# Six experts' token tiles turned by VectorE blocks of 32x32 in place of TensorE transposes

## The chip, the cores and the metric

The kernel runs on one core of a Trainium2 chip. The metric is device time in microseconds (us) of one execution. Engines are named as in the profile: PE is TensorE (matmuls; PEld its weight loads), DVE is VectorE, ACT is ScalarE, POOL is GpSimd, SP is the queue of SyncE that issues most DMAs. POOL issues the indirect DMAs (gathers and scatters of rows by a list of row numbers).

## The reference, cut to what matters

```python
def reference(q, k, v, p, ...):
    a = sm_attn(q, pp, pp), pp = sm_attn(p, k, v)        # 4 batches, 8 heads, 576 tokens, 64 wide
    x = a.transpose(...).reshape(2304, 512)
    x = sum over 4 experts of p[:, e] * (relu(x @ w1[e]) @ w2[e])          # dense, 1024 hidden
    logits = x @ w_gate + log1p(exp(x @ w_noise)) * noise                  # 8 experts
    top2, weights = the two largest of 8 per token, softmax over the two
    out[token] = sum over its 2 experts of weight * (relu(x @ m1[e]) @ m2[e])
```

The change lies in the last line: each of 8 experts is run on the tokens that chose it, some 576 of 2304 on average, in a list with room for 640 (`cap`), which is 5 tiles of 128 tokens (`T2`).

## The kernel before, in words

The first 700 us are attention, the dense experts and the routing. Routing leaves in DRAM a table `meta` with one row of 4 numbers for each slot of each expert (token, weight, and two row numbers), and `x2d`, the tokens' rows of 512 numbers. The stage that the change touches is the rest of the span, the eight routed experts.

The work of this stage is cut into parts j (`subs`): expert 0 in two parts, then j = 2 is expert 1, and j = 3 to 8 are experts 2 to 7. Each part has 8 steps f, one for 128 hidden units. In a step, PE first runs `e_mm1` of the next step (24 matmuls: hidden units from the tokens' columns, two halves of 320 tokens) and then `e_mm2` of this one (15 matmuls: 5 tiles of tokens into 5 accumulators). Every product is three matmuls (`mm3`, lines 63 to 65), since numbers are split in a high part (tags ending in h) and a low part (l): ACT copies the rounded high part, and DVE or POOL subtracts it from the original (`split`, lines 68 and 69). Hidden units leave PSUM by `evac_h` (lines 468 and 469), ACT for `gh`, DVE for `gl`. Weights come as 512 KB tiles `raw` on SP, and are split into `w1h`, `w1l` and `w2h`, `w2l`: for most of the experts' weights ACT does the high and POOL the low part; DVE does the low part of some of the first ones (the list `first`).

Beside this, for the next part, `gather` (line 780) has POOL fetch 5 tiles of 128 rows of `x2d` into `xg`; and `xg_t` (line 793), for one tile in each of five steps, turns a tile over by 4 TensorE transposes (line 798) into a PSUM buffer `mm`, from which ACT and DVE split it into `xth`, `xtl`. The tile in step 6 of a part is the last one that the next part's `e_mm1` needs, and that `e_mm1` follows right behind step 6 on PE. POOL also clears (`gt`, line 804) and fills (line 808, from `yd`) the tile of what the tokens' first expert gave, and at a part's end scatters the results `y` to the output (line 851).

What goes into each engine's queue, and in which order, is set by hand: `at(place, f, ...)` gives every piece of side work a place between the PE steps, and `run` issues them there. Each engine works through its queue in order. The row numbers for the gathers come from `mt_load` (a DMA of the `meta` rows on SP) and `mt_index` (three DVE copies to integers).

Of the kernel before, what the change touches and what calls it, by code (L numbers as in the profile page):

```python
# [22 lines left out]
CH, NC = 128, 5  # L23
BIG = 65536.0
CAP = 640


@with_exitstack
def tile_pack_attn_moe_moe(ctx: ExitStack, tc: tile.TileContext, qT, kT, pT, vv, dp, noise,
# [108 lines left out]
    def at(place, f, *a):  # L138
        fill.append((place, len(fill), f, a))
# [6 lines left out]

    TM, S2 = 200, 300

    def weights(key, tag, bufs, src, load, cut):
        at(cut + 0.10, w_split, key, tag, bufs)  # L150
        at(load + 0.11, w_load, key, src)

    def w1_src(e, d):
# [580 lines left out]
    def mt_load(e0, e1, t0, t1):  # L734
        n = len(mt_i)
        m = rtp.tile([128, e1 - e0, t1 - t0, 4], F32, name="mt", tag=f"mt{n}", bufs=1)
        r0, r1 = e0 * cap + t0 * 128, (e1 - 1) * cap + t1 * 128
        ins = nc.sync.dma_start(m.rearrange("p e t c -> p (e t) c"),
                                meta[r0:r1, :].rearrange("(x p) c -> p x c", p=128))
        ix = rtp.tile([128, 3, e1 - e0, t1 - t0], I32, name="mti", tag=f"mti{n}", bufs=1)  # L740
        mt_i[n] = 0
        return m, ix, ins

    def mt_index(m, ix):
        for i, c in enumerate((0, 2, 3)):
            nc.vector.tensor_copy(ix[:, i], m[:, :, :, c])

    MT = {}

    def mt_w(e, t):  # L750
        m, _, a, b = MT[e, t]
# [13 lines left out]
    def mt_late():  # L765
        m, ix, _ = mt_load(0, 1, tA, T2)
        at(S2 + 4.1, mt_index, m, ix)
        for t in range(tA, T2):
            MT[0, t] = (m, ix, 0, t - tA)
        at(S2 + 5.3, mt_rest, 1, 2, S2 + 6.9)  # L770
        at(S2 + 13.0, mt_rest, 2, E2, S2 + 15.2)

    def mt_rest(e0, e1, place):
        m, ix, _ = mt_load(e0, e1, 0, T2)
        at(place, mt_index, m, ix)
        for e in range(e0, e1):
            for t in range(T2):
                MT[e, t] = (m, ix, e - e0, t)

    def gather(j):  # L780
        e, t0, n = subs[j]
        rows = 13 * 128 if j == 0 else NTOK
        XG[j] = [(xgp if j == 0 else mo).tile([128, 512], F32, name="xg", tag="xg", bufs=tA if j == 0 else T2)
                 for _ in range(n)]
        for t in range(n):
            ins = nc.gpsimd.indirect_dma_start(
                out=XG[j][t], out_offset=None, in_=x2d[0:rows, :],
                in_offset=bass.IndirectOffsetOnAxis(ap=mt_ix(e, t0 + t, 0), axis=0),
                bounds_check=rows - 1, oob_is_err=False)
            if j == 0:  # L790
                early_rows.append(ins)

    def xg_t(j, t):
        if t == 0:
            XT[j] = [mo.tile([128, 4, cap], F32R, name=f"xt{z}", tag=f"xt{z}", bufs=2) for z in "hl"]
        o = mm_ps()
        for d in range(4):
            nc.tensor.transpose(o[:, d * 128:(d + 1) * 128], XG[j][t][:, d * 128:(d + 1) * 128], ident)  # L798
        h, l = [z[:, :, t * 128:(t + 1) * 128] for z in XT[j]]
        split(h, l, o.rearrange("p (d j) -> p d j", d=4))  # L800

    def g_zero(e):
        Gt[e] = mo2.tile([128, T2, 512], F32, name="gt", tag="gt", bufs=1)
# [69 lines left out]
        n_over.append(nc.values_load(n_over[0][0:1, 0:1], min_val=0, max_val=NTOK))  # L873

    at(TM + 21, mt_early)
    at(TM + 26.5, gather, 0)
    for t in range(tA):
        at(TM + 36 + t, xg_t, 0, t)
    at(S2 + 2.6, mt_late)
    at(S2 + 4.12, gather, 1)  # L880
    for t in range(T2 - tA):
        at(S2 + 6.05 + t / 10, xg_t, 1, t)
    at(S2 + 10.1, count_over)
    for j in range(1, len(subs)):
        s = S2 + 8 * j
        e = subs[j][0]
        if j + 1 < len(subs):
            at(s + 0.13 if j > 1 else S2 + 7.0, gather, j + 1)
            for t in range(T2):
                at(s + 2.13 + t, xg_t, j + 1, t)  # L890
            at(s + 8.13, y_store, e)
        if e > 0:
            at(s + 2.14, g_zero, e)
            at(s + 3.14, g_load, e)
# [59 lines left out]
    with tc.If(rv > 0):  # L954
        with tc.tile_pool(name="sl", bufs=2) as sl:
            with tc.For_i(0, NT, 1) as i:
                x = sl.tile([128, 512], F32, name="sx")
                nc.sync.dma_start(x, x2d[ds(i * 128, 128), :])
                gw = sl.tile([128, E2], F32, name="sg")
                nc.sync.dma_start(gw, gwd[ds(i * 128, 128), :])  # L960
                di = sl.tile([128, 1], I32, name="sd")
                nc.sync.dma_start(di, sdd[ds(i * 128, 128), :])
                o = mm_ps()
                for d in range(4):
                    nc.tensor.transpose(o[:, d * 128:(d + 1) * 128], x[:, d * 128:(d + 1) * 128], ident)
                xt = sl.tile([128, 4, 128], F32, name="sxt")
                nc.scalar.activation(xt, o.rearrange("p (d j) -> p d j", d=4), AF.Copy)
                r = sl.tile([128, 512], F32, name="sr")
                nc.vector.memset(r, 0.0)
                for e in range(E2):  # L970
                    a = acc_ps()
                    for fp in range(4):
# [12 lines left out]
                nc.gpsimd.indirect_dma_start(out=out, out_offset=bass.IndirectOffsetOnAxis(ap=di[:, :1], axis=0),  # L985
                                             in_=r, in_offset=None, bounds_check=NTOK - 1, oob_is_err=False)


def layouts(q, k, v, p, moe_domain_probs, moe_w1, moe_w2, moe2_w_gate, moe2_w_noise, moe2_noise, moe2_w1, moe2_w2):
# [3 lines left out]
    def heads(a):  # L993
# [12 lines left out]
        ("m1", moe2_w1.reshape(E2, 4, 128, 4, 2, 128).transpose(0, 3, 2, 4, 1, 5).reshape(E2, 4, 128, 1024)),  # L1006
# [28 lines left out]
```

## Time and profile before

| | |
|---|---|
| time, median of 3 | 1237.41 us (1234.49 to 1237.69) |
| the profiled execution's own time | 1236.17 us |
| its span in the trace | 1234.3 us |
| granted TensorE clock, mean | 0.986 of full speed |
| PE busy | 1191.7 us, 97% |
| DVE, ACT, POOL busy | 437.4, 396.3 and 392.3 us |

The span runs from the first to the last instruction on the core; the execution's own time has 1.9 us more around it. The busy time of PE is modelled from pipelined instructions, so 97% says that something is always in it, not that it works at its peak.

### The profile page before, as it was taken

Reading aid. Unit: us, or ns where it says so; the run is one execution under the profiler, and the core shown is the slowest. Engines: PE = TensorE matmul, PEld = TensorE weight load, DVE = VectorE, ACT = ScalarE, POOL = GpSimd, SP = SyncE. Lnnn points to the kernel's source line nnn. Section 1 sums busy time; section 2 is a strip of 40 time slices with the busy share of each in tenths; the row PEclk is TensorE's granted clock in tenths of the full one; section 3 lists DMA queues with packets and bytes.
Section 4 is the critical chain, followed back from the end, with each engine's and each line's share of the span. In section 5 each row is a group of like instructions: output and inputs, shape, how many; then the busy total and the mean of one; then the engine's idle time right before and its main releaser. Section 6 shows DMA issues by size and latency. Waiting matters only on the chain.

```text
span 1234.3 us, 18214 instructions
## 1 busy us (share of the span) xinstructions
PE 1191.7 (97%) x7328; PEld 999.9 (81%) x7328; DVE 437.4 (35%) x1111; ACT 396.3 (32%) x848; POOL 392.3 (32%) x272
## 2 busy tenths in 40 slices
PE   6889999999999999999999988899999999999997
PEld 2668788778788888788887976689998998899986
DVE  5452343333545212633332635441222222222222
ACT  2432422323324324323223523242232323232321
POOL 0110200201203101116102143326565665757464
PEclk7999999999999999999999998899999999999999
DMA  7212131213122211301600235563344343535342
GB/s 290 100 49 116 35 111 65 77 35 112 55 104 78 74 64 35 103 1 36 104 18 18 77 90 96 131 194 99 118 138 141 111 164 111 179 98 199 100 143 78
DMA packets 50953, 121.79 MB, mean 99 GB/s; under 512 B 17658, under 2 KB 18058, under 8 KB 50864
## 3 DMA queue, kind: packets, MB, share of 16 engines
q1 hardware_dynamic: 40864, 100.46, 26.2%
q0 software_dynamic: 10000, 20.11, 5.1%
q8 instruction: 60, 0.98, 0.3%
q14 instruction: 29, 0.24, 0.1%
HBM read 106.13 MB, written 23.31 MB: 105 GB/s over the span
## 4 chain that ended last, share of the span: by engine, by line
PE 83%; DMA 6%; DVE 5%; issue 2%; ACT 2%; POOL 1%; SPq 0%; POOLq 0%; DVEq 0%; ACTq 0%
PE acc L63 13%; PE acc L64 13%; PE acc L65 13%; PE mm L63 10%; PE mm L64 10%; PE mm L65 10%; PE mm L343 2%; PE accx L63 2%; PE accx L64 2%; PE accx L65 2%; DMA gt<-yd,mti 2%; DMA meta<-rr,rsi 2%; PE mm L798 1%; DMA raw<-in_m_dram 1%; DVE ta L305 0%
## 5 line engine op out<-in xcount | busy, mean ns | idle before, releaser
L69 POOL TENSOR_TENSOR w2l<-raw,w2h 128x1024 fp32r<-128x1024 f32 x61 | 146.3, 2399 | 480.8 <-ACT w2h L68 480.5
L63 PE MATMUL acc<-w2h,hh 128*128 128x512 f32 x448 | 184.5, 412 | 0.0
L64 PE MATMUL acc<-w2l,hh 128*128 128x512 f32 x448 | 178.1, 398 | 0.0
L65 PE MATMUL acc<-w2h,hl 128*128 128x512 f32 x448 | 176.9, 395 | 0.0
L63 PE MATMUL mm<-ath,mh 128*128 128x288 f32 x512 | 153.8, 300 | 6.8 <-ACT ath L68 4.0
L63 PE MATMUL mm<-xth,w1h 128*128 128x320 f32 (+2 forms) x512 | 159.3, 311 | 0.1
L64 PE MATMUL mm<-xtl,w1h 128*128 128x320 f32 (+2 forms) x512 | 158.7, 310 | 0.3 <-DVE xtl L69 0.3
L65 PE MATMUL mm<-xth,w1l 128*128 128x320 f32 (+2 forms) x512 | 158.3, 309 | 0.0
L469 DVE SCALAR_TENSOR_TENSOR gl<-mm,gh 128x320 fp32r<-128x320 f32 (+2 forms) x128 | 62.8, 491 | 266.0 <-ACT gh L468 241.6
L469 DVE SCALAR_TENSOR_TENSOR hl<-mm,hh 128x224 fp32r<-128x224 f32 (+1 forms) x256 | 104.2, 423 | 147.8 <-ACT hh L468 144.8
L65 PE MATMUL mm<-ath,ml 128*128 128x288 f32 x512 | 151.3, 296 | 2.8 <-DVE ml L350 2.8
L64 PE MATMUL mm<-atl,mh 128*128 128x288 f32 x512 | 151.9, 297 | 0.5 <-DVE atl L69 0.4
L468 ACT ACTIVATE gh<-mm 128x320 fp32r<-128x320 f32 (+2 forms) x128 | 56.0, 437 | 285.1 <-PE mm L65 251.2
L468 ACT ACTIVATE hh<-mm 128x224 fp32r<-128x224 f32 (+1 forms) x256 | 93.3, 384 | 136.1 <-PE mm L65 105.4
L63 PEld LDWEIGHTS acc<-w2h,hh 128*128 128x128 f32 x448 | 84.1, 188 | 45.1 <-issue 29.0
L63 PE MATMUL acc<-w2h,gh 128*128 128x512 f32 x264 | 108.6, 411 | 5.7 <-ACT gh L468 5.7
L63 PEld LDWEIGHTS mm<-ath,mh 128*128 128x128 f32 x512 | 96.2, 188 | 17.9 <-ACT ath L68 6.2
L65 PE MATMUL acc<-w2h,gl 128*128 128x512 f32 x264 | 106.1, 402 | 2.1 <-DVE gl L469 2.0
L64 PE MATMUL acc<-w2l,gh 128*128 128x512 f32 x264 | 105.4, 399 | 0.0
L64 PEld LDWEIGHTS mm<-atl,mh 128*128 128x128 f32 x512 | 96.5, 188 | 6.1 <-DVE atl L69 0.9
L65 PEld LDWEIGHTS acc<-w2h,hl 128*128 128x128 f32 x448 | 84.3, 188 | 20.7
L63 PEld LDWEIGHTS mm<-xth,w1h 128*128 128x128 f32 x512 | 96.8, 189 | 3.8 <-ACT xth L68 0.4
(238 smaller groups left out, 1906.2 us busy)
## 6 DMA issues: line engine op xcount, KB each, us to landing
raw<-in_m_dram SPq DMA_DIRECT2D x72, 512.0 KB
raw<-in_w_dram SPq DMA_DIRECT2D x32, 512.0 KB
yd<-y SPq DMA_DIRECT2D x7, 1280.0 KB
w1h<-in_w_dram SPq DMA_DIRECT2D x16, 512.0 KB
w1l<-in_w_dram SPq DMA_DIRECT2D x16, 512.0 KB
v<-in_vv_dram SPq DMA_DIRECT2D x8, 640.0 KB
qk<-in_kT_dram SPq DMA_DIRECT2D x8, 576.0 KB
qk<-in_qT_dram SPq DMA_DIRECT2D x8, 576.0 KB
```

The source lines that it names most:

```text
L63: nc.tensor.matmul(o, ah, bh, start=start, stop=False)
L64: nc.tensor.matmul(o, ah, bl, start=False, stop=False)
L65: nc.tensor.matmul(o, al, bh, start=False, stop=stop)
L69: (eng or nc.vector).tensor_sub(l, x, h.bitcast(F32))
L343: nc.tensor.matmul(o[h2][hp * 32:hp * 32 + 32, :], PT[bb][r, hp, :], w, start=True, stop=True)
L468: nc.scalar.activation(hd, src, AF.Relu)
L469: nc.vector.scalar_tensor_tensor(ld, src, 0.0, hd.bitcast(F32), op0=OP.max, op1=OP.subtract)
L798: nc.tensor.transpose(o[:, d * 128:(d + 1) * 128], XG[j][t][:, d * 128:(d + 1) * 128], ident)
```

## The change

For experts 2 to 7 (`EN` = 2) a tile is gathered as four columns of quarter rows: `x2d` is seen as 9216 rows of 128 numbers, and gather b of a tile brings, to partition 32 q + i, quarter q of the token in slot 32 b + i. Four gathers of 128 rows of 512 B take the place of one of 128 rows of 2 KB. One DVE transpose of 32x32 blocks then puts the tile into the form that `e_mm1` needs, except that the rows of the contraction are permuted, which the host's layout of `m1` follows. ACT and DVE split it from SBUF (`xq`), not from PSUM.

The numbers of the quarter rows, 4 times the token plus q, are made once for all six experts: 16 small matmuls with columns of the identity put the token of slot 32 b + i on all partitions 32 q + i, and one DVE instruction multiplies by 4 and adds `quarter`. For this the load of the `meta` rows of experts 2 to 7 is placed earlier (S2 + 8.0, was S2 + 13.0), and its index instructions at S2 + 11.5 (was 15.2). The gathers of a part are placed one tile in each step, not five at once. The low parts of the weights that the second `weights` loop handles (50 tiles, from the last quarter of expert 1's on) move from POOL to DVE. A branch for tokens beyond the room of 640 is adapted as well.

```diff
+        nc.gpsimd.iota(jp, pattern=[[0, 128]], base=0, channel_multiplier=1)
+        nc.vector.tensor_scalar(jp, jp, 5, None, op0=OP.logical_shift_right)
+        nc.vector.tensor_copy(quarter, jp[:, 0:1])
...
-                weights(("m1", j, d), "w1", 2, m1[subs[j][0], d], n - 4, n - 3)
-                weights(("m2", j, d), "w2", 4, m2[subs[j][0], d], n - 3, n - 2)
+                weights(("m1", j, d), "w1", 2, m1[subs[j][0], d], n - 4, n - 3, vec)
+                weights(("m2", j, d), "w2", 4, m2[subs[j][0], d], n - 3, n - 2, vec)
...
+    def mt_index(m, ix, iq=None, eng=vec):
         for i, c in enumerate((0, 2, 3)):
+            eng.tensor_copy(ix[:, i], m[:, :, :, c])
+        if iq is not None:
+            o = mm_ps()
+            x = iq.shape[2]
+            for b in range(4):
+                for q in range(4):
+                    nc.tensor.matmul(o[q * 32:q * 32 + 32, b * x:(b + 1) * x], ident[:, b * 32:b * 32 + 32],
+                                     m.rearrange("p e t c -> p (e t) c")[:, :, 0], start=True, stop=True)
+            nc.vector.tensor_scalar(iq, o[:, :4 * x].rearrange("p (b x) -> p b x", b=4), 4.0, quarter,
+                                    op0=OP.mult, op1=OP.add)
...
-        at(S2 + 13.0, mt_rest, 2, E2, S2 + 15.2)
+        at(S2 + 8.0, mt_rest, 2, E2, S2 + 11.5)
...
+            iq, at_ = IQ[e]
+            for b in range(4):
+                nc.gpsimd.indirect_dma_start(
+                    out=XG[j][t][:, b * 128:(b + 1) * 128], out_offset=None,
+                    in_=x2d.rearrange("t (q d) -> (t q) d", q=4),
+                    in_offset=bass.IndirectOffsetOnAxis(ap=iq[:, b, at_ + t:at_ + t + 1], axis=0),
+                    bounds_check=4 * NTOK - 1, oob_is_err=False)
...
+        x = mo.tile([128, 4, 4, 32], F32, name="xq", tag="xq", bufs=2)
+        nc.vector.transpose(x.rearrange("p b d j -> p (b d j)"), XG[j][t])
+        split(*[z.rearrange("p d (b j) -> p d b j", b=4) for z in (h, l)], x.rearrange("p b d j -> p d b j"))
...
-            at(s + 0.13 if j > 1 else S2 + 7.0, gather, j + 1)
             for t in range(T2):
+                at(s + 0.13 + t if j > 1 else S2 + 7.0, gather, j + 1, (t,))
                 at(s + 2.13 + t, xg_t, j + 1, t)
```

POOL's queue over one of the experts 2 to 6, before (`w1l`, `w2l` are weight splits, `out_dram` the scatters, `xg` the gathers of tokens, `gt` the clearing and the gathers of earlier results):

```order
L851 DMA out_dram<-y,mti 2304x512 x2
L69 TENSOR_TENSOR w1l<-raw,w1h 128x1024
L851 DMA out_dram<-y,mti 2304x512 x3
L69 TENSOR_TENSOR w2l<-raw,w2h 128x1024
L786 DMA xg<-x2d,mti 128x512 x5
L69 TENSOR_TENSOR w1l<-raw,w1h 128x1024
L69 TENSOR_TENSOR w2l<-raw,w2h 128x1024
L804 MEMSET gt 128x2560
L69 TENSOR_TENSOR w1l<-raw,w1h 128x1024
L808 DMA gt<-yd,mti 128x512 x5
L69 TENSOR_TENSOR w2l<-raw,w2h 128x1024
```

The same stretch of POOL's queue in the changed kernel:

```order
L889 DMA out_dram<-y,mti 2304x512 x5
L819 DMA xg<-x2d,iq 128x128 x12
L842 MEMSET gt 128x2560
L819 DMA xg<-x2d,iq 128x128 x4
L846 DMA gt<-yd,mti 128x512 x5
L819 DMA xg<-x2d,iq 128x128 x4
```

The eight weight splits of an expert are gone from this queue, 5 gathers have become 20, and the last tile's 4 gathers now stand behind the clearing and the 5 gathers of `gt`.

DVE's queue in the changed kernel, from step 5 of an expert over step 6 to its end (`STREAM_TRANSPOSE` is the block transpose; before, a step had its two `gl` and one `xtl`):

```order
L476 SCALAR_TENSOR_TENSOR gl<-mm,gh 128x320 x2
L71 TENSOR_TENSOR w1l<-raw,w1h 128x1024
L837 STREAM_TRANSPOSE xq<-xg 128x512
L71 TENSOR_TENSOR xtl<-xq,xth 128x4x128
L476 SCALAR_TENSOR_TENSOR gl<-mm,gh 128x320 x2
L71 TENSOR_TENSOR w2l<-raw,w2h 128x1024
L837 STREAM_TRANSPOSE xq<-xg 128x512
L71 TENSOR_TENSOR xtl<-xq,xth 128x4x128
L476 SCALAR_TENSOR_TENSOR gl<-mm,gh 128x320 x2
L888 SCALAR_TENSOR_TENSOR y<-acc,mt,gt 128x512 x2
L71 TENSOR_TENSOR w1l<-raw,w1h 128x1024
L888 SCALAR_TENSOR_TENSOR y<-acc,mt,gt 128x512 x2
```

A split and a block transpose now stand in each step between the `gl` of one step and those of the next.

SP's queue around the load of the `meta` rows of experts 2 to 7 (`mt`, 128x30x4) in the changed kernel; before, it stood five rows further down, behind the fifth of the `raw` loads that follow it here:

```order
L745 DMA mt_7493<-meta_75 128x5x4
L132 DMA raw_7545<-in_m1_dram 128x1024
L132 DMA raw_7601<-in_m2_dram 128x1024
L745 DMA mt_7624<-meta_75 128x30x4
L132 DMA raw_7636<-in_m1_dram 128x1024
L132 DMA raw_7665<-in_m2_dram 128x1024
```

The load now goes out between two loads of weights for the second part of expert 0.

## Rows read from the trace of the kernel before

**Rows 1.** Part 1 of the page: busy time, share of span, instructions by engine.

```profile
PE 1191.7 (97%) x7328; PEld 999.9 (81%) x7328; DVE 437.4 (35%) x1111; ACT 396.3 (32%) x848; POOL 392.3 (32%) x272
```

**Rows 2.** Timeline of DVE, one expert: start, duration, instruction, idle time before it.

```profile
951.53 0.49 DVE L469 SCALAR_TENSOR_TENSOR gl<-mm,gh 128x320 fp32r<-128x320 f32 x1 [4.76 <-ACT gh L468]
...
958.55 0.49 DVE L469 SCALAR_TENSOR_TENSOR gl<-mm,gh 128x320 fp32r<-128x320 f32 x1 [4.77 <-ACT gh L468]
...
965.99 0.49 DVE L469 SCALAR_TENSOR_TENSOR gl<-mm,gh 128x320 fp32r<-128x320 f32 x1 [3.00 <-ACT gh L468]
...
990.06 0.49 DVE L469 SCALAR_TENSOR_TENSOR gl<-mm,gh 128x320 fp32r<-128x320 f32 x1 [1.26 <-ACT gh L468]
...
995.75 0.49 DVE L469 SCALAR_TENSOR_TENSOR gl<-mm,gh 128x320 fp32r<-128x320 f32 x1 [3.00 <-ACT gh L468]
```

**Rows 3.** Timeline of PE, same expert: a tile's four transposes, and step 6's first e_mm2.

```profile
983.35 0.60 PE L798 MATMUL mm<-ident,xg 128*128 128x128 f32 x4
...
989.39 0.39 PE L63 MATMUL acc<-w2h,gh 128*128 128x512 f32 x1
```

**Rows 4.** The chain that ended last: start us, us, what.

```profile
13.82 0.81 PE mm L271 x40
...
784.62 5.12 DMA xg<-x2d,mti
...
800.62 4.29 DMA raw<-in_m_dram
...
807.25 0.35 DVE gl L469
```

**Rows 5.** Timeline, 784 to 803 us: POOL's gathers and DVE's splits.

```profile
784.62 1.90 POOL L786 DMA_INDIRECT xg<-x2d,mti  x1 [10.93 <-DVE mti L746]
...
786.82 1.01 POOL L786 DMA_INDIRECT xg<-x2d,mti  x1 [0.31 <-issue]
787.55 1.22 DVE L69 TENSOR_TENSOR w2l<-raw,w2h 128x1024 fp32r<-128x1024 f32 x1 [1.47 <-ACT w2h L68]
...
799.38 1.22 DVE L69 TENSOR_TENSOR w2l<-raw,w2h 128x1024 fp32r<-128x1024 f32 x1
799.64 1.82 POOL L786 DMA_INDIRECT xg<-x2d,mti  x1 [0.30 <-issue]
...
801.48 1.23 DVE L69 TENSOR_TENSOR w1l<-raw,w1h 128x1024 fp32r<-128x1024 f32 x1 [0.52 <-ACT w1h L68]
801.76 1.81 POOL L786 DMA_INDIRECT xg<-x2d,mti  x1 [0.30 <-issue]
```

**Rows 6.** Groups by line, shapes apart: count | busy us, mean ns | idle before.

```profile
L69 DVE TENSOR_TENSOR xtl<-mm,xth 128x512 fp32r<-128x512 f32 x40 | 27.6, 691 | 53.6 <-ACT xth L68 50.6 <-issue 3.0
...
L325 DVE STREAM_TRANSPOSE tb<-ta 128x576 f32<-128x576 f32 x7 | 5.4, 774 | 0.4 <-POOL ta L317 0.2
```

**Rows 7.** Timeline of ACT, step 6 of the expert of rows 2.

```profile
989.93 1.05 ACT L68 ACTIVATE w2h<-raw 128x1024 fp32r<-128x1024 f32 x1
991.43 0.60 ACT L68 ACTIVATE xth<-mm 128x512 fp32r<-128x512 f32 x1 [0.45 <-PE mm L798]
```

**Rows 8.** Timeline, start of expert 1, while expert 2's tokens are fetched.

```profile
829.80 0.49 DVE L469 SCALAR_TENSOR_TENSOR gl<-mm,gh 128x320 fp32r<-128x320 f32 x1 [1.27 <-ACT gh L468]
830.80 2.38 POOL L69 TENSOR_TENSOR w2l<-raw,w2h 128x1024 fp32r<-128x1024 f32 x1 [7.88 <-ACT w2h L68]
```

**Rows 9.** Timeline of POOL, the expert of rows 2.

```profile
940.70 1.03 POOL L851 DMA_INDIRECT out_dram<-y,mti  x1 [5.48 <-DVE y L850]
...
963.64 2.24 POOL L804 MEMSET gt<- 128x2560 f32 x1
```

**Rows 10.** Windows: busy us by engine (instructions), granted clock, DMA share, GB/s.

```profile
801.00:807.00 6.00, 6.00 (x41) 5.18 (x40) 2.63 (x3) 2.16 (x4) 2.27 (x2) 1.00 0.82 283
807.00:808.00 1.00, 0.94 (x9) 0.71 (x9) 0.82 (x4) 0.38 (x1) 0.00 (x0) 1.00 0.00 0
817.00:823.00 6.00, 6.00 (x43) 5.66 (x42) 2.37 (x5) 3.01 (x5) 2.40 (x1) 1.00 0.85 155
```

More of the change, by code (lines that the diff above doesn't have):

```diff
@@ L25 @@
 CAP = 640
+EN = 2
 @with_exitstack
@@ L81, in tile_pack_attn_moe_moe @@
     cnt = consts.tile([128, 8], F32, name="cnt")
+    quarter = consts.tile([128, 1], F32, name="quarter")
     nov = consts.tile([128, NT], BF, name="nov")
@@ L147, in tile_pack_attn_moe_moe, with weights @@
     TM, S2 = 200, 300
-    def weights(key, tag, bufs, src, load, cut):
-        at(cut + 0.10, w_split, key, tag, bufs)
+    def weights(key, tag, bufs, src, load, cut, eng=None):
+        at(cut + 0.10, w_split, key, tag, bufs, eng)
         at(load + 0.11, w_load, key, src)
@@ L741, in mt_load @@
         mt_i[n] = 0
+        if e0 >= EN:
+            iq = rtp.tile([128, 4, (e1 - e0) * T2], I32, name="iq", tag=f"iq{n}", bufs=1)
+            for e in range(e0, e1):
+                IQ[e] = (iq, (e - e0) * T2)
+            return m, ix, ins, iq
         return m, ix, ins
-    def mt_index(m, ix):
+    def mt_index(m, ix, iq=None, eng=vec):
         for i, c in enumerate((0, 2, 3)):
-            nc.vector.tensor_copy(ix[:, i], m[:, :, :, c])
-    MT = {}
+            eng.tensor_copy(ix[:, i], m[:, :, :, c])
[8 more added lines that the diff above has]
+                                    op0=OP.mult, op1=OP.add)
+    MT, IQ = {}, {}
     def mt_w(e, t):
@@ L770, in mt_late @@
         at(S2 + 5.3, mt_rest, 1, 2, S2 + 6.9)
-        at(S2 + 13.0, mt_rest, 2, E2, S2 + 15.2)
+        at(S2 + 8.0, mt_rest, 2, E2, S2 + 11.5)
     def mt_rest(e0, e1, place):
-        m, ix, _ = mt_load(e0, e1, 0, T2)
-        at(place, mt_index, m, ix)
+        m, ix, _, *quarters = mt_load(e0, e1, 0, T2)
+        at(place, mt_index, m, ix, *quarters)
         for e in range(e0, e1):
@@ L778, in mt_rest, with gather @@
                 MT[e, t] = (m, ix, e - e0, t)
-    def gather(j):
+    def gather(j, ts):
         e, t0, n = subs[j]
         rows = 13 * 128 if j == 0 else NTOK
[L783 to L791, printed above, removed]
+        if ts[0] == 0:
+            XG[j] = [(xgp if j == 0 else mo).tile([128, 512], F32, name="xg", tag="xg", bufs=tA if j == 0 else T2)
+                     for _ in range(n)]
+        for t in ts:
+            if e < EN:
+                ins = nc.gpsimd.indirect_dma_start(
+                    out=XG[j][t], out_offset=None, in_=x2d[0:rows, :],
+                    in_offset=bass.IndirectOffsetOnAxis(ap=mt_ix(e, t0 + t, 0), axis=0),
+                    bounds_check=rows - 1, oob_is_err=False)
+                if j == 0:
+                    early_rows.append(ins)
+                continue
+            iq, at_ = IQ[e]
[5 more added lines that the diff above has]
+                    bounds_check=4 * NTOK - 1, oob_is_err=False)
     def xg_t(j, t):
@@ L795, in xg_t @@
             XT[j] = [mo.tile([128, 4, cap], F32R, name=f"xt{z}", tag=f"xt{z}", bufs=2) for z in "hl"]
-        o = mm_ps()
-        for d in range(4):
-            nc.tensor.transpose(o[:, d * 128:(d + 1) * 128], XG[j][t][:, d * 128:(d + 1) * 128], ident)
         h, l = [z[:, :, t * 128:(t + 1) * 128] for z in XT[j]]
-        split(h, l, o.rearrange("p (d j) -> p d j", d=4))
+        if subs[j][0] < EN:
+            o = mm_ps()
+            for d in range(4):
+                nc.tensor.transpose(o[:, d * 128:(d + 1) * 128], XG[j][t][:, d * 128:(d + 1) * 128], ident)
+            split(h, l, o.rearrange("p (d j) -> p d j", d=4))
+            return
+        x = mo.tile([128, 4, 4, 32], F32, name="xq", tag="xq", bufs=2)
+        nc.vector.transpose(x.rearrange("p b d j -> p (b d j)"), XG[j][t])
+        split(*[z.rearrange("p d (b j) -> p d b j", b=4) for z in (h, l)], x.rearrange("p b d j -> p d b j"))
     def g_zero(e):
@@ L875, in tile_pack_attn_moe_moe @@
     at(TM + 21, mt_early)
-    at(TM + 26.5, gather, 0)
+    at(TM + 26.5, gather, 0, range(tA))
     for t in range(tA):
@@ L879, in tile_pack_attn_moe_moe @@
     at(S2 + 2.6, mt_late)
-    at(S2 + 4.12, gather, 1)
+    at(S2 + 4.12, gather, 1, range(T2 - tA))
     for t in range(T2 - tA):
@@ L962, in tile_pack_attn_moe_moe @@
                 nc.sync.dma_start(di, sdd[ds(i * 128, 128), :])
[L963 to L967, printed above, removed]
+                xo = sl.tile([128, 512], F32, name="sxo")
+                nc.vector.tensor_copy(xo.rearrange("p (d q j) -> p d q j", d=4, q=4),
+                                      x.rearrange("p (q d j) -> p d q j", d=4, q=4))
+                xts = []
+                for z, y in enumerate((x, xo)):
+                    o = mm_ps()
+                    for d in range(4):
+                        nc.tensor.transpose(o[:, d * 128:(d + 1) * 128], y[:, d * 128:(d + 1) * 128], ident)
+                    xt = sl.tile([128, 4, 128], F32, name=f"sxt{z}")
+                    nc.scalar.activation(xt, o.rearrange("p (d j) -> p d j", d=4), AF.Copy)
+                    xts.append(xt)
                 r = sl.tile([128, 512], F32, name="sr")
@@ L971, in tile_pack_attn_moe_moe @@
                     a = acc_ps()
+                    xt = xts[e >= EN]
                     for fp in range(4):
@@ L1005, in layouts @@
         ("w2", moe_w2.reshape(E1, 8, 128, 512).transpose(0, 2, 1, 3)),
-        ("m1", moe2_w1.reshape(E2, 4, 128, 4, 2, 128).transpose(0, 3, 2, 4, 1, 5).reshape(E2, 4, 128, 1024)),
+        ("m1", np.concatenate([
+            moe2_w1[:EN].reshape(EN, 4, 128, 4, 2, 128).transpose(0, 3, 2, 4, 1, 5).reshape(EN, 4, 128, 1024),
+            moe2_w1[EN:].reshape(E2 - EN, 4, 4, 32, 4, 2, 128).transpose(0, 4, 1, 3, 5, 2, 6)
+            .reshape(E2 - EN, 4, 128, 1024)])),
         ("m2", moe2_w2.reshape(E2, 4, 2, 128, 512).transpose(0, 1, 3, 2, 4).reshape(E2, 4, 128, 1024)),
```

## The prediction

> **What bounds the kernel now.** I read the page's first part first: PE is busy for 97% of the span and no other engine for more than 35% [rows 1]. That only says where to look. The second view is the timeline of one of the experts 2 to 6 in its steady state. Each step leaves a pair of gl instructions on DVE, so the distance between the same gl of two neighbouring steps is the length of a step. Two steps without a tile to turn are 958.55 - 951.53 = 7.02 us apart, and the next, with a tile's four transposes, 965.99 - 958.55 = 7.44 us [rows 2]. DVE idles 3.00 to 4.77 us before these rows and waits there for ACT, which waits for PE. So in this stage PE alone sets the length of a step, and work taken from PE shortens it until something else is late.
>
> **What is removed from PE.** The trace gives the four transposes of a tile 0.60 us [rows 3], but that overlaps with the matmuls around them. The step lengths hold what they really cost: 7.44 - 7.02 = 0.42 us for a tile. Experts 2 to 7 have 6 x 5 = 30 tiles: 30 x 0.42 = 12.7 us (0.424 unrounded). All of these steps lie in the stage where PE is the bound, so this comes off the end if nothing takes its place.
>
> **What is added on PE.** 16 small matmuls for the quarter rows, once. The trace has no such form; the nearest is a run of 40 matmuls on 32 columns, 0.81 us [rows 4], which would make 0.32 us for 16. From above I take the transposes' 0.42 us for four, so 1.7 us. They are nearer to the first form: 0.5 us.
>
> **What DVE takes over.** In each step one weight split, 1.22 us [rows 5], and one block transpose, 0.69 us by the row of 774 ns for 576 columns [rows 6] scaled to 512; the low part of the tile stays at 0.69 us, from SBUF now. The 1.9 us more fit into idle time of 3.00 and 1.26 us per step [rows 2]. Nor is a late gl a loss at once: the gl of a step are read by the matmuls that follow after the next e_mm1, and three PSUM buffers, which the tiles no longer share, hold the halves. I cost it at nothing. Without that cover it would be 1.9 us in each of the 30 steps with a tile, 57 us.
>
> One place has less room, step 6 of an expert, whose tile the next expert's e_mm1 reads at once. In the frame of rows 2 the second gl of step 6 starts at 990.06 - 4 x 0.42 = 988.35 (four of the expert's tiles stand before it). The split behind it waits for its ACT half, which ends 0.92 us after that start (989.93 + 1.05 - 990.06) [rows 7], and ends by 990.5. Then follow transpose (0.69), ACT's copy (0.60 [rows 7]) and xtl (0.69), with hand-overs between them: 992.6. PE's first half of that e_mm1 needs only the first 320 columns; by the distance of 995.75 - 990.06 - 0.42 = 5.27 us between the gl, less the 0.67 us that a gl starts after PE went on to the next matmul (990.06 - 989.39 [rows 2, 3]), the second half starts at 992.95. There are 0.35 us to spare, so nothing is lost if the tile itself is there by 990.5.
>
> **POOL's queue.** It loses 50 splits of 2.4 us [rows 8], 120 us, and gains 90 gathers of 1.01 + 0.30 us [rows 5], 118 us. The load does not change, the order does. An expert now has 30 transfers of 1.31 us and 2.24 us of clearing, 41.6 us of a step time of 8 x 7.02 = 56.1. What counts is when the last tile's fourth gather is done. From the first scatter at 940.70 [rows 9]: 5 scatters to 947.25, 12 gathers to 963.0, clearing to 965.3, 4 gathers to 970.5, 5 gathers of gt to 977.1, 4 gathers to 982.3. A gather landed 5.12 us after the start of an instruction of 1.90 us [rows 4, 5], 3.2 us after its end, so the tile lands at 985.2 to 985.5; needed at 990.5. That leaves 5.1 us.
>
> Now the wait that this trace shows. A gather that begins while DVE runs a split, an instruction with both inputs in SBUF, takes 1.82 and 1.81 us, in both rows to 0.86 us behind the split's end (the one of 1.90 is the same case); one that began 0.73 us before a split took 1.01 [rows 5]. So each split can hold up one gather, by 0 to 1.0 us. In the changed kernel DVE runs one such split in each step, and xtl has both inputs in SBUF too. Until the last gather six splits and three xtl fall in POOL's stream; at random phase some 0.6 us for a split and 0.2 for an xtl, 4.2 us, at most 6 x 1.0 + 3 x 0.6 = 7.8, at least 0. With 4.2 of 5.1 us used, an expert in the steady state loses nothing; at 7.8 it loses 2.7 - 0.35 = 2.3 us. I take 0 for these five.
>
> [...]
>
> Expert 2 starts later on POOL: two splits of expert 1's weights stay there. A split runs to 833.2 [rows 8]; then 4 gathers, the other split of 2.4, 8 gathers, the clearing, 4 gathers, 5 of gt and 4 gathers end at 870.5 and land at 873.7. Needed: the second gl of step 0 stands at 829.80 [rows 8], that of step 6 is 6 x 7.02 later, and 2.15 us on (as 988.35 to 990.5 above) is 874.1. Only 0.4 us are left, and three splits and three xtl hold POOL up for 2.4 us (0 to 4.8). The tile is 2.0 us late, of which 0.35 are spare: I take 1.6 us on PE, with 0 and 4.1 as bounds.
>
> **The load of the meta rows** goes out behind the raw load of 800.62 [rows 4], not within the stretch from 817 to 823. In that stretch the DMA engines were 0.85 busy for 155 GB/s, where 283 GB/s made 0.82 [rows 10]; so the load's small pieces take about (0.85 - 0.45) x 6 = 2.4 us of all engines. Moved, they meet a stretch that is 0.82 full, and the chain runs through it: that raw load, its split, and PE waits until a gl at 807.25 [rows 4]. That raw load is ahead in the queue; the next one can be up to 2.4 us later, but the engines are idle at 807 to 808 [rows 10], and it has to wait for ACT anyway. I take 0.5 us, bounds 0 and 2.4. PE's products stand three and a half steps further on in its queue.
>
> **At nothing:** the constants (three short instructions, made once among attention's work; without cover less than 1 us), the gathers' traffic (the same bytes in smaller pieces, in steps that wait for no DMA [rows 2]; a late one is the case above), and the branch for overflow, which is not run.
>
> **Sum.** -12.7 + 0.5 + 1.6 + 0.5 = -10.1 us. Against the profiled execution's own 1236.2 us that is 1226.1; the median shown is 1.2 us above it. I say 1226.5 us, between the two.
>
> **Rivals.**
> - No hold-up on POOL: -12.7 + 0.5 + 0.5 = -11.7, 1224.5 us. For it: a gather that began before a split was not held up; against it: the two that began inside one [rows 5]. Chance 0.17.
> - POOL late in part of the experts: at the upper bound of the splits' cost, 2.3 us in each of five experts and 4.1 in expert 2, so -12.7 + 1.0 + 15.6 = +3.9, 1240 us; at half of that, 1232. For it: DVE and POOL are both tied to PE's steps, so the phase can be the bad one in every expert. Chance 0.17, of which two thirds stay faster.
> - POOL as the bound, slower: place, the last tile's gathers behind gt; if also the block transposes hold up gathers, or a gather of quarter rows takes 1.8 us throughout, POOL needs 10 x 1.31 + 20 x 2.1 + 2.3 = 57.4 us for an expert, over 56.1; the last tile is 11 us late or more, in 6 experts 66 us, 1290; from 8 us of delay in an expert (5.1 + 0.35 + 12/5) the change loses. Chance 0.07. A lesser form: each gather waits for the eighth POOL transfer before it, which 10 us cover now.
> - The change does not shorten the steps, because something else holds them at 7.44, so 1236: against it the steps of 7.02 us in the same expert, with the same loads [rows 2]. Chance 0.04: no change.
>
> **How the numbers follow.** The forecast (1225 to 1229) has 0.55. About 0.3% (3.7 us) is what a measurement of this kernel can tell from no change. Faster: 0.55 + 0.17 + 0.11 = 0.83. Same: 0.04 + 0.04 = 0.08. Slower: 0.07 + 0.02 = 0.09. The range runs from 1222 (the rival without hold-up, less the 2.9 us by which the runs' lowest lies under their median) to 1235 (the second rival's middle and somewhat more), and leaves out 0.07 to 0.15 above.
>
> **What would show it right or wrong.** Right: 40 of the 160 TensorE transposes of tiles are left, and all steps of experts 2 to 6 are 7.02 us apart; POOL's gathers number 130, some of 1.8 us where a DVE split runs; the block transpose takes 0.7 us and waits for a DMA only in expert 1's step 6. Wrong: a wait of that transpose for xg in every expert, then PE idle at the next expert's first matmuls; gathers of quarter rows over 1.3 us; or PE idle at 801 to 812 us, behind a raw load.

## The result, and the profile after

The changed kernel takes 1217.9 us (median of 4, 1215.62 to 1219.53) against 1236.22 us for the kernel before beside it (median of 4, 1234.49 to 1237.69): a ratio of 0.9851, 95% interval 0.9828 to 0.9874, so 18 us faster. I had forecast 1226.5 us and a range of 1222 to 1235. The direction was right; the size was nearly twice the forecast and lies below the range.

The first part of the page, busy time and its share by engine, answers to [rows 1]:

```profile
PE 1170.9 (96%) x7240; PEld 986.8 (81%) x7240; DVE 519.3 (43%) x1194; ACT 397.5 (33%) x848; POOL 382.7 (31%) x313
```

PE has lost 21 us of busy time and stays the bound; DVE has gained 82 us. The groups of shapes for the operations that were moved (busy us, mean ns of one, idle before it):

```profile
L819 POOL DMA_INDIRECT xg<-x2d,iq x120 | 136.4, 1136 | 35.4 <-issue 33.5 <-DMA xg<-x2d,iq 1.8
L837 DVE STREAM_TRANSPOSE xq<-xg 128x512 f32<-128x512 f32 x30 | 21.1, 704 | 0.0
L71 DVE TENSOR_TENSOR xtl<-xq,xth 128x512 fp32r<-128x512 f32 x30 | 20.8, 693 | 21.0 <-ACT xth L70 21.0
L832 PE MATMUL mm<-ident,xg 128*128 128x128 f32 x40 | 7.6, 322 | 4.1 <-DMA xg<-x2d,mti 3.2 <-DVE xtl L71 1.0
```

The block transpose takes 0.704 us and never waits for its tile (0.0 us idle ahead of it); 40 TensorE transposes are left. The timeline of DVE in an expert of the steady state answers to [rows 2]; the second `gl` of each step:

```profile
945.95 0.49 DVE L476 SCALAR_TENSOR_TENSOR gl<-mm,gh 128x320 fp32r<-128x320 f32 x1 [1.21 <-ACT gh L475]
...
952.89 0.49 DVE L476 SCALAR_TENSOR_TENSOR gl<-mm,gh 128x320 fp32r<-128x320 f32 x1 [1.27 <-ACT gh L475]
...
966.77 0.49 DVE L476 SCALAR_TENSOR_TENSOR gl<-mm,gh 128x320 fp32r<-128x320 f32 x1 [1.21 <-ACT gh L475]
967.72 1.23 DVE L71 TENSOR_TENSOR w2l<-raw,w2h 128x1024 fp32r<-128x1024 f32 x1 [0.46 <-ACT w2h L70]
968.86 0.70 DVE L837 STREAM_TRANSPOSE xq<-xg 128x512 f32<-128x512 f32 x1
970.26 0.69 DVE L71 TENSOR_TENSOR xtl<-xq,xth 128x512 fp32r<-128x512 f32 x1 [0.70 <-ACT xth L70]
...
973.71 0.49 DVE L476 SCALAR_TENSOR_TENSOR gl<-mm,gh 128x320 fp32r<-128x320 f32 x1 [1.21 <-issue]
```

Here is what the forecast did not have. The step with a tile is as short as one without, as forecast, but both are 6.94 us (952.89 - 945.95, 973.71 - 966.77), not 7.02. Steps without a tile, in which nothing was taken from PE, became 0.08 us shorter too. The place is in the timeline of PE, in a step of the last expert, which had no tiles to turn before either: the first of the 15 matmuls of `e_mm2`, and the first matmul behind them. Before:

```profile
1185.58 0.39 PE L63 MATMUL acc<-w2h,gh 128*128 128x512 f32 x1
...
1189.08 0.31 PE L63 MATMUL mm<-xth,w1h 128*128 128x320 f32 x1
```

After:

```profile
1188.18 0.39 PE L65 MATMUL acc<-w2h,gh 128*128 128x512 f32 x1
...
1191.61 0.30 PE L65 MATMUL mm<-xth,w1h 128*128 128x320 f32 x1
```

The 15 matmuls take 3.50 us before and 3.43 after, at a granted clock of 1.00 in both. In the experts (930 to 1190 us) the next matmul starts 0.2328 us after a 512-column one on average before and 0.2284 after, and in the dense stage (100 to 700 us), which the diff does not touch, 0.2349 and 0.2327; distances over 0.26 us, which are waits or missing records, are left out of these means. For the 320-column matmuls it is 0.1465 us in both. The diff touches neither these matmuls nor their data. But it adds the constant `quarter`, 4 bytes in each partition, ahead of the weight tiles: in the built program `w2h` begins at byte 45504 of a partition before, and at 45536 after.

### The profile page after: what moved, and what is told of

Its sections match the earlier page's. It is cut to its first block, busy times and chain, and to the rows that moved or that the text cites. A ratio compares the mean times of both kernels' runs of the same rounds, so it can differ in the third digit from the quotient of the medians.

```text
span 1215.4 us, 18241 instructions
## 1 busy us (share of the span) xinstructions
PE 1170.9 (96%) x7240; PEld 986.8 (81%) x7240; DVE 519.3 (43%) x1194; ACT 397.5 (33%) x848; POOL 382.7 (31%) x313
## 4 chain that ended last, share of the span: by engine, by line
PE 82%; DMA 8%; DVE 6%; ACT 2%; issue 1%; POOL 0%; SPq 0%; POOLq 0%; DVEq 0%; ACTq 0%
PE acc L65 13%; PE acc L66 13%; PE acc L67 13%; PE mm L65 11%; PE mm L67 10%; PE mm L66 10%; DMA gt<-yd,mti 3%; PE mm L350 2%; PE accx L65 2%; PE accx L66 2%; PE accx L67 2%; DMA meta<-rr,rsi 2%; DMA raw<-in_m_dram 1%; DMA yd<-y 1%; DVE ta L312 0%
## 5 line engine op out<-in xcount | busy, mean ns | idle before, releaser
L71 POOL TENSOR_TENSOR w2l<-raw,w2h 128x1024 fp32r<-128x1024 f32 x36 | 86.3, 2396 | 431.2 <-ACT w2h L70 421.9
L819 POOL DMA_INDIRECT xg<-x2d,iq x120 | 136.4, 1136 | 35.4 <-issue 33.5
L65 PE MATMUL acc<-w2h,gh 128*128 128x512 f32 x264 | 105.2, 399 | 5.4 <-ACT gh L475 5.4
```

Source lines behind the costliest of these rows:

```text
L65: nc.tensor.matmul(o, ah, bh, start=start, stop=False)
L71: (eng or nc.vector).tensor_sub(l, x, h.bitcast(F32))
L819: nc.gpsimd.indirect_dma_start(out=XG[j][t][:, b * 128:(b + 1) * 128], out_offset=None, in_=x2d.rearrange("t (q d) -> (t q) d", q=4), in_o ...
```

## The experiments

Each ran beside the kernel before, and ratios are to that; its median was 1229.5 to 1232.9 us in these rounds, against 1236.2 beside the changed kernel, so kernels of different rounds are compared by their ratios. The changed kernel itself was not run again. "Spacing" is the mean distance defined above, worked out from the starts in each trace. My theory was that the 32 bytes shortened the matmuls' spacing; the rivals were that GpSimd's splits had widened it before, and that the two profiled executions differ by chance.

**The address alone.** e1 is the kernel before with one unused constant:

```diff
     cnt = consts.tile([128, 8], F32, name="cnt")
+    pad = consts.tile([128, 1], F32, name="pad")
```

> The kernel before with one unused constant of 4 bytes per partition, which moves all weight tiles by 32 bytes in SBUF, as the quarter constant of the change does. Theory A (the address of the weight tiles sets the spacing of 512-column matmuls): in the experts they stand 0.227 us apart instead of 0.2325, 15 of them in a step, 64 steps: 5.3 us; in the dense stage the trace of after had gained 4.0 us between 103 and 702 us: together 8 to 9 us, so 1227 to 1228 us. Theory B (the gain comes from the weight splits that left GpSimd) and theory C (the difference is one of single executions): no change, 1236 us.

Measured: 1225.55 us against 1231.21, ratio 0.9956 (0.9941 to 0.9970), 5.4 us faster, with not one operation of the change in it. The spacing fell to 0.2332 us in the dense stage and to 0.2299 in the experts. In the timeline of DVE the steps of the last two experts, first two with a tile and then two without:

```profile
1137.69 0.49 DVE L471 SCALAR_TENSOR_TENSOR gl<-mm,gh 128x320 fp32r<-128x320 f32 x1 [2.98 <-ACT gh L470]
...
1145.11 0.49 DVE L471 SCALAR_TENSOR_TENSOR gl<-mm,gh 128x320 fp32r<-128x320 f32 x1 [2.99 <-ACT gh L470]
...
1180.77 0.49 DVE L471 SCALAR_TENSOR_TENSOR gl<-mm,gh 128x320 fp32r<-128x320 f32 x1 [4.69 <-ACT gh L470]
...
1187.71 0.49 DVE L471 SCALAR_TENSOR_TENSOR gl<-mm,gh 128x320 fp32r<-128x320 f32 x1 [4.69 <-ACT gh L470]
```

The step without a tile is 6.94 us, as after; the one with a tile 7.42 (7.02 and 7.44 before). So the address explains the shorter step in full, and at the new address a tile's transposes cost 0.48 us, not 0.42. Theory A holds, though for 5.4 us and not for the 8 to 9 us that I had expected: in the experts the spacing did not reach 0.2284, and in the dense stage it is 0.2332 where the changed kernel has 0.2327.

**Other causes for the spacing.** e3 moves only the weight splits of the kernel before to VectorE, e16 adds to e1 4096 unused bytes that put the `g` and `x` tiles where they stand after, e17 is e1 and e3 together.

```diff
-                weights(("m1", j, d), "w1", 2, m1[subs[j][0], d], n - 4, n - 3)
+                weights(("m1", j, d), "w1", 2, m1[subs[j][0], d], n - 4, n - 3, vec)
... (m2 likewise; and in e16, in xg_t:)
+            nc.gpsimd.memset(mo.tile([128, 1024], F32, name="gpad", tag="gpad", bufs=1), 0.0)
```

> The kernel before with the weight splits of experts 2 to 7 on VectorE, all else as before. Theory A: steps of 7.02 us without a tile and 7.44 with one stay, 1235 to 1237 us. Theory B: steps without a tile of 6.94 us, about 4 us less, 1232 us.

Measured: 0.9997 (0.9985 to 1.0009), spacing 0.2328. Moving the splits off GpSimd gains nothing here.

> The kernel before with the 4 unused bytes ahead of the weight tiles (0.9956) and 4096 unused bytes ahead of the g and x tiles, so that these stand at the addresses of the changed kernel too. If addresses explain the rest: 512-column matmuls 0.2284 us apart in the experts instead of 0.2299, 960 x 0.0015 = 1.4 us less, 0.9945 of before. If something else of the change does (GpSimd's splits gone): 0.2299 and 0.9956.

Measured: 0.9963 (0.9951 to 0.9975), spacing 0.2299: no effect.

> The kernel before with the 4 unused bytes ahead of the weight tiles and with the weight splits of experts 2 to 7 on VectorE. If GpSimd's splits widened the spacing: 512-column matmuls 0.2284 us apart in the experts, some 1.4 us less than with the 4 bytes alone, 0.9945 of before. If not: 0.2299 and 0.9956 to 0.9963.

Measured: 0.9981 (0.9968 to 0.9993), spacing 0.2299. Neither was the cause of the step from 0.2299 to 0.2284. That step goes with the transposes: from 1166 to 1190 us, in the last expert, which has none, the spacing is 0.2286 in e1 and in the changed kernel alike. The three padded kernels, 0.9956, 0.9963 and 0.9981, together put the address at 2 to 5 us in the kernel before.

**The change without its address.** e2 puts `quarter` behind the weight tiles, so that these stay where they were before:

```diff
-    quarter = consts.tile([128, 1], F32, name="quarter")
...
+    quarter = rtp.tile([128, 1], F32, name="quarter")
```

> The changed kernel with the quarter constant behind the weight tiles, so that these stand at the addresses of before. Theory A: it loses 8 to 9 us against the changed kernel, 1226 to 1227 us, with steps of 7.02 us in the experts: the forecast's number. Theory B or C: 1218 us, steps of 6.94 us.

Measured: 1269.71 us, ratio 1.0307 (1.0280 to 1.0335). Neither theory had that. The timeline of PE, in a step of an expert:

```profile
958.98 0.40 PE L67 MATMUL accx<-w2h,gl 128*128 128x512 f32 x1
960.17 0.40 PE L65 MATMUL mm<-xth,w1h 128*128 128x320 f32 x1 [0.80 <-issue]
960.41 0.30 PE L66 MATMUL mm<-xtl,w1h 128*128 128x320 f32 x1
961.59 0.43 PE L67 MATMUL mm<-xth,w1l 128*128 128x320 f32 x1 [0.87 <-issue]
962.31 0.62 PE L65 MATMUL mm<-xth,w1h 128*128 128x320 f32 x1 [0.30 <-issue]
963.04 0.61 PE L66 MATMUL mm<-xtl,w1h 128*128 128x320 f32 x1
964.43 0.62 PE L67 MATMUL mm<-xth,w1l 128*128 128x320 f32 x1 [0.78 <-issue]
```

PE starts a matmul only every 0.7 to 1.4 us (now and then two stand 0.2 us apart) and waits for nothing that the profile shows. The first gathers of neighbouring experts stand 64.6 to 68.7 us apart in place of eight steps, 56.1: an expert is 8 to 13 us longer. Part of that is a lower clock: in the windows of 5 us from 960 and 965 us, in which PE idled 2.23 and 1.57 us, 0.66 and then 0.50 of full speed was granted, and from 968.2 to 971.4 us the 320-column matmuls stood 0.27 us apart, against 0.147 us from 952.2 to 955.3. PE had started the last matmul of a half at 953.81, but ACT's copy of this half begins only at 963.08:

```profile
963.08 0.44 ACT L475 ACTIVATE gh<-mm 128x320 fp32r<-128x320 f32 x1 [12.80 <-remote]
```

The semaphore of PE that ACT waits for is updated at 963.00 in the trace's record, so PE's signal came late as well. The spacing is 0.2332 us again. At this point the price of the change alone could not be read; I sought the cause of the pauses first.

**Which program pauses.** e5 is the changed kernel with 224 unused bytes ahead of the weight tiles, which gives them the address of before modulo 256; e8 is e2 once more, loaded anew; e6 is e2 with e1's `pad`.

```diff
+    pad = consts.tile([128, 56], F32, name="pad")
```

> The changed kernel with 224 unused bytes per partition ahead of the weight tiles, so that their addresses stand modulo 256 where those of before and of the kernel of 1269.7 us stand (192). Theory A (alignment sets the spacing of the 512-column matmuls): 0.2328 us apart in the experts instead of 0.2284, some 4 us slower than the changed kernel, 0.989 of before. Theory D (the long pauses of PE in the kernel of 1269.7 us come from weight tiles at this alignment together with gathers of quarter rows): 1.03 of before. Theory E (they come from where that one program was placed when it was loaded): no pauses, 0.989.

Measured: 1.0259 (1.0228 to 1.0291), the same pauses. The spacing in the experts is 0.2332 us, as at the old address, though this kernel has one constant more than the changed one: it is the address that counts, not the constant.

> The kernel of 1269.7 us once more, loaded anew. Theory D: 1.03 of before again, with the same pauses of PE. Theory E: 0.99, without pauses.

Measured: 1.0315 (1.0281 to 1.0350), the same pauses: not the luck of one load.

> The kernel of 1269.7 us with 4 unused bytes per partition ahead of the weight tiles (at the addresses of the changed kernel again); the quarter constant stays behind them. Theory D: no pauses, as the changed kernel, 0.985 of before. Theory E: cannot be told ahead; a second load of almost the same program, most likely without pauses. If the place of the quarter constant itself mattered: 1.03.

Measured: 1.0021 (0.9985 to 1.0058), its executions spread from 1225 to 1246 us; in the trace, which is that of the slowest, two experts pause and three don't, at the weight addresses of the changed kernel, so theory D in its simple form falls. The experts of one trace could then be compared. The timeline of POOL in e2, from the last scatter on, in an expert that pauses:

```profile
949.03 0.98 POOL L889 DMA_INDIRECT out_dram<-y,mti  x1 [0.30 <-issue]
950.32 1.04 POOL L819 DMA_INDIRECT xg<-x2d,iq  x1 [0.30 <-issue]
951.66 1.02 POOL L819 DMA_INDIRECT xg<-x2d,iq  x1 [0.31 <-issue]
```

And in the changed kernel, which doesn't pause:

```profile
938.76 0.98 POOL L889 DMA_INDIRECT out_dram<-y,mti  x1 [0.30 <-issue]
940.04 2.05 POOL L819 DMA_INDIRECT xg<-x2d,iq  x1 [0.30 <-issue]
942.40 1.01 POOL L819 DMA_INDIRECT xg<-x2d,iq  x1 [0.31 <-issue]
```

In the traces so far the first gather was held up, to some 2.05 us, where a weight split on DVE began 0.06 to 0.09 us ahead of it, and ran in 1.04 us where the split began less than 0.04 us ahead or later. Every expert in them with a held-up first gather was free of long pauses (0.7 us at most), and each of the others paused.

**Moving that gather.** e9 puts the clearing of `gt` ahead of the first gather, e10 a small clearing, both in e2; e11 moves the split, in e4 below.

```diff
-            at(s + 2.14, g_zero, e)
+            at(s + 0.125, g_zero, e)
... (e10 instead:)
+                if t == 0 and j > 1:
+                    at(s + 0.125, pause)      # nc.gpsimd.memset(pd, 0.0), 128x256
... (e11:)
-                weights(("m2", j, d), "w2", 4, m2[subs[j][0], d], n - 3, n - 2, vec)
+                weights(("m2", j, d), "w2", 4, m2[subs[j][0], d], n - 3, n - 2 + (0.25 if d == 1 else 0), vec)
```

> The kernel of 1269.7 us with the clearing of gt (2.25 us on GpSimd) ahead of an expert's first gather instead of behind the twelfth; GpSimd's work stays the same. In all experts seen so far PE paused where the first gather ran in 1.04 us beside a weight split, and did not where the split held it up to 2.05 us. Theory H (the hold-up itself is what prevents the pauses): the first gather now starts after the split's end and is not held up, so pauses, 1.03 of before. Theory L (the gathers start too early, while the store of y fills the DMA engines; a later start prevents the pauses): none, steps of 7.02 us, 0.99 of before.

Measured: 1218.01 us, 0.9906 (0.9889 to 0.9922), no pause. The first gather (939.42) took 1.04 us without a hold-up, so theory H falls.

> The kernel of 1269.7 us with a clearing of 256 columns on GpSimd (some 0.25 us) ahead of each expert's first gather, so that this gather starts inside the weight split and is held up to some 2 us. Theories H and L: no pauses, steps of 7.02 us, 0.99 of before. If the pauses have nothing to do with this gather: 1.03.

Measured: 1217.90 us, 0.9906 (0.9890 to 0.9923), no pause; the first gather was held up to 1.95 us. A clearing of 0.34 us on an engine with time to spare was worth some 50 us. **These two are the change without its address**: 0.9906, 11.6 us of 1236, where I had forecast 10.1. The clearing that is added or moved in them does not make that number: e14 below, without it, gives 0.9900, and e12 with it 0.9846 against 0.9837 for e4. Steps are 7.02 us in the timeline of e9, as forecast:

```profile
957.40 0.49 DVE L476 SCALAR_TENSOR_TENSOR gl<-mm,gh 128x320 fp32r<-128x320 f32 x1 [1.21 <-ACT gh L475]
...
964.42 0.49 DVE L476 SCALAR_TENSOR_TENSOR gl<-mm,gh 128x320 fp32r<-128x320 f32 x1 [1.21 <-ACT gh L475]
```

> The fastest kernel so far (the changed kernel with the meta load at its place of before, 1210.9 us, no pauses) with the one weight split that meets each expert's first gather placed two to three tiles later, so that the gather is not held up. Theories H and L: pauses of 6 to 10 us of PE in each expert, 1.02 to 1.04 of before. If the pauses come from tile addresses alone: none, 0.984.

Measured: 0.9847 (0.9826 to 0.9869), but the edit did not move the split in time (the gather was still held up, 2.05 us): it tells nothing.

e14 issues the store of `y`, which runs beside these gathers, one step later, in e2. e15 delays the split by an ACT copy of 8 columns ahead of it, in e4. e18 has the same copy in e2.

```diff
-            at(s + 8.13, y_store, e)
+            at(s + 9.13, y_store, e)
```

> The kernel of 1269.7 us with the store of y issued one step later, behind the first five gathers or so. Theory L in the form that the gathers meet the store: no pauses at the first gathers, 0.99 of before, or pauses at another place. If the store has no part in it: pauses as before, 1.03.

Measured: 0.9900 (0.9882 to 0.9918), no pause, though the first gathers start at once and run in 1.03 us. The store has a part in it.

```diff
     def w_split(key, tag, bufs, eng=None):
+        if key[0] == "m2" and key[1] > 2 and key[2] == 1:
+            nc.scalar.activation(wait, cnt, AF.Copy)
```

> The changed kernel with the meta load at its place of before (no pauses, 0.984 of before) and a copy of 8 columns, some 0.2 us, on ACT ahead of the copy that leads to the weight split beside each expert's first gather from expert 3 on. The split then starts after the gather and does not hold it up. Theory L: pauses of PE of 6 to 10 us in each of these experts, 1.015 to 1.03 of before. If the hold-up of the first gather has no part in it: 0.984 to 0.985.

Measured: 0.9852 (0.9833 to 0.9872). The first gather ran in 1.03 us beside the split, 3.0 us behind the issue of the store as in e2, and PE did not pause:

```profile
935.80 1.03 POOL L822 DMA_INDIRECT xg<-x2d,iq  x1 [0.30 <-issue]
935.82 1.23 DVE L71 TENSOR_TENSOR w2l<-raw,w2h 128x1024 fp32r<-128x1024 f32 x1 [0.55 <-ACT w2h L70]
```

So theory L as I had it falls too: that meeting is not enough.

> The kernel of 1269.7 us with the copy of 8 columns on ACT ahead of the weight split beside each expert's first gather from expert 3 on; the split then starts some 0.1 us later against the gather. If the weight tiles' addresses decide (with gathers that are not held up): pauses as before, 1.03 of before. If the phase of split and gather within some hundredths of a us decides: none, 0.990.

Measured: 1.0378 (1.0315 to 1.0441), pauses in experts 2 to 6. So the copy ahead of the split is not what ends the pauses in e15 (the split starts 0.02 us after the gather there, 0.09 to 0.11 here). e15 and e18 also differ in the addresses of the weight tiles and of `quarter` and in the place of the meta load; which of these decides, if one does, is open, for e7 below pauses at the weight addresses of e15 and with its meta load.

**The moved meta load, and a faster kernel.** e4 is the changed kernel with `mt_rest` at its places of before.

```diff
-        at(S2 + 8.0, mt_rest, 2, E2, S2 + 11.5)
+        at(S2 + 13.0, mt_rest, 2, E2, S2 + 15.2)
```

> The changed kernel with the load of the meta rows of experts 2 to 7 and its index work at their places of before. My forecast priced the move at 0.5 us (bounds 0 and 2.4): 1217.4 us. The trace of after shows PE idle for 1.5 us between 800 and 810 us, where it was busy throughout before: by that 1216.4 us. If the move cost nothing, 1217.9.

Measured: 0.9837 (0.9820 to 0.9853), 1.7 us below 0.9851 by the middles; the intervals overlap. The trace of the changed kernel shows what is gone here; busy us of each engine in windows, clock, DMA share and GB/s:

```profile
795.00:800.00 5.00, 5.00 (x33) 4.49 (x32) 3.28 (x5) 1.72 (x3) 3.64 (x3) 1.00 0.94 274
800.00:805.00 5.00, 4.22 (x30) 3.54 (x29) 2.40 (x5) 1.93 (x3) 0.00 (x0) 1.00 0.96 185
805.00:810.00 5.00, 4.23 (x58) 3.60 (x57) 2.68 (x4) 2.88 (x4) 0.67 (x1) 1.00 0.49 137
```

The DMA engines are 0.96 full for 185 GB/s from 800 to 805 us, the raw loads come late (ACT waits 2.37 and 2.30 us for them), and from 800 to 810 us PE idles 1.55 us. In e4's windows from 790 to 810 us PE idles 0.06 us.

e7 adds to e4 128 unused bytes ahead of the `h` tiles, which give the dense stage's `h` and `w2` tiles the same address modulo 256, as `g` and `w2` have after the change. e12 is e4 with e9's edit, e13 has all three.

```diff
     dpt = rtp.tile([128, NT, E1], F32, name="dpt")
+    hpad = rtp.tile([128, 32], F32, name="hpad")
```

> The changed kernel with the meta load at its place of before and 128 unused bytes ahead of the dense stage's h tiles, so that h and weight tiles have the same address modulo 256 in the dense stage as g and weight tiles have in the experts. If that offset sets the spacing (0.2329 us in the dense stage at an offset of 128, 0.2284 in the experts at 0): 1728 matmuls x 0.0045 = 7.8 us faster than without it, 0.977 of before. If the dense stage's spacing has another cause: 0.984, as without it.

Measured: 0.9975 (0.9948 to 1.0003), executions from 1220 to 1246 us. The dense spacing did fall, to 0.2291 us, but four of the experts paused in the trace, which is that of the slowest execution.

> The fastest kernel so far with the clearing of gt ahead of each expert's first gather. Theory L: no pauses, 0.984 of before or a little less, and not by luck of some hundredths of a us any more. Theory H: pauses, 1.02 to 1.04.

Measured: 0.9846 (0.9822 to 0.9870), no pause.

> The changed kernel with three edits together: the meta load at its place of before, 128 unused bytes ahead of the h tiles, the clearing of gt ahead of each expert's first gather. With the 128 bytes alone the dense stage's 512-column matmuls stood 0.2291 us apart instead of 0.2328, but pauses of PE in the experts cost more than that. Theory L: no pauses, 1728 x 0.0037 = 6.4 us less than 0.9846 of before, so 0.979 to 0.980. If the pauses come from these addresses: 0.99 or more.

Measured: 1204.79 us, **0.9797** (0.9783 to 0.9811), no pause: faster than before and than the changed kernel. The groups of its dense matmuls, whose means were 410 and 394 ns in the changed kernel and 412 and 398 before:

```profile
L65 PE MATMUL acc<-w2h,hh 128*128 128x512 f32 x448 | 182.8, 408 | 0.0
L66 PE MATMUL acc<-w2l,hh 128*128 128x512 f32 x448 | 176.2, 393 | 0.0
```

These durations overlap and show little of it; the spacing (0.2328 to 0.2291 over 1728 matmuls, 6.4 us) is what counts.

## Why the prediction was wrong in its size

**The step that failed** is the sentence "At nothing: the constants". I priced the three instructions that make `quarter` and not the 4 bytes that move every weight tile by 32 (`w2h` from 45504 to 45536). From the same cause "all steps of experts 2 to 6 are 7.02 us apart" failed: 6.94. The changed kernel (0.9851) against e9 and e10 (0.9906) puts this at 0.0055, 6.8 us, the larger part of the 8.3 us by which the forecast's 10.1 fell short of 18.4 (0.0149 of 1236). That is a difference of two rounds and uncertain by some 3.5 us, by the two intervals; in the traces alone, the stretch from expert 2's first `gl` to the end is 14.4 us shorter than before in the changed kernel and 11.0 in e9.

**Steps with a tile: -12.7 us.** Right. In e9 an expert takes eight steps of 7.02 us, in place of 7.44 for five of them. At the new address, by e1's steps, the same 30 tiles are worth 30 x 0.48 = 14.4 us.

**POOL's queue.** Right in its course; but the kernel was free of pauses by luck, for the forecast had nothing of the pauses of PE that came in e2, where each expert that paused had its first gather run in 1.04 us without a hold-up. The last tile's last gather in the steady state:

```profile
933.50 1.03 POOL L889 DMA_INDIRECT out_dram<-y,mti  x1 [10.96 <-DVE y L888]
...
977.06 1.00 POOL L819 DMA_INDIRECT xg<-x2d,iq  x1 [0.30 <-issue]
```

It ends 44.6 us after the first scatter; I had 41.6 (982.3 - 940.7) and 4.2 for hold-ups. Those measured are 2.05, 1.36, 1.41, 1.91, 1.42 and 1.42 us in place of 1.0: 3.6. DVE's splits do hold up gathers (up to 2.05 us against 1.0), and nothing waits for it, as I took it; what in the chip holds a gather up no run here shows.

**Expert 2's last tile: +1.6 us.** Wrong: it cost nothing. The last split on POOL before these gathers began at 828.96, not so late as to end at 833.2; hold-ups cost 1.35 us, not 2.4; and the tile was there sooner. The gather ends at 869.62, and the transpose follows the split at 871.70 without a wait:

```profile
870.56 1.23 DVE L71 TENSOR_TENSOR w2l<-raw,w2h 128x1024 fp32r<-128x1024 f32 x1 [0.46 <-ACT w2h L70]
871.70 0.70 DVE L837 STREAM_TRANSPOSE xq<-xg 128x512 f32<-128x512 f32 x1
```

**The meta load: +0.5 us.** The mechanism was right, the size too small: PE idles 1.55 us behind late raw loads at 804 and 809 us, inside the bounds of 0 to 2.4 but nearer the upper one. e4 agrees with 1.7 us, within the noise.

**The small matmuls: +0.5 us.** Two records for each of the 16; all start between 807.5 and 807.9 us. About right.

The forecast's own terms as measured, -12.7 for the steps, 1.6 for the meta load, 0.5 for the small matmuls and nothing for expert 2's last tile, make -10.6 us against 11.6 measured in e9 and e10. That the sum of -10.1 came so near is in part luck: the term for the tile was 1.6 too much and that for the meta load 1.1 too little. The address is worth 2 to 5.4 us in e1, e16 and e17, and 30 x (0.48 - 0.42) = 1.8 more for tiles that are worth more there: 4 to 7 us, against the 6.8 between e9 and e10 and the changed kernel.

**The rivals.** "No hold-up" has about the time of e9 and e10 but not their mechanism. "POOL late" and "POOL as the bound" did not come; a slower kernel was near all the same, by pauses of PE, of which the trace of before shows nothing.

## What to carry to other kernels

Before a difference is put down to the operations that were edited, compare the distance between matmuls that were not: a new constant of 4 bytes moved this kernel by 2 to 5 us and its changed form by 6.8. Look up which tiles an edit shifts, and where a forecast rests on a step length, say that it holds for one layout. When a change lands well, see on what it stands: here each expert's first gather began 0.07 to 0.09 us behind a split and was held up, and in six kernels of nearly the same program PE paused where it was not. A clearing placed ahead of it costs nothing that the runs can tell (0.9846 against 0.9837), and no kernel that had one paused.

## What the runs showed of the hardware

- The distance between 512-column matmuls changed with the place of their tiles in SBUF: 0.2332 us (e9) with `w2` at byte 192 and `g` at 224 modulo 256, 0.2284 (the changed kernel) with both at 224; in the dense stage, for `w2` and `h`, 0.2349 (192 and 96), 0.2332 (224 and 128, e1), 0.2327 (224 and 96), 0.2325 (192 and 64, e5) and 0.2291 (both 224, e13). Both addresses count, then; what in the chip makes the difference is not shown. With 320 columns it stayed 0.1465 us in kernels without pauses.
- PE paused with nothing to wait for in the profile, starting one matmul in 0.7 to 1.4 us (e2); there an expert was 8 to 13 us longer by it. It happened only where the first gathers of quarter rows ran beside the split and the store of `y` without a hold-up (26 experts of six kernels), and was gone where the first gather came 2.1 us later, or 0.2 us later and then was held up, or where the store came one step later; but five experts of e15 met in the same way and did not pause. What in the chip holds PE then was not found.
